# In the second group of quarter tiles, w2 of the second next tile is requested behind a visit at an iteration's fourth hook

## The chip, the cores and the metric

The kernel runs on one core of a Trainium2 chip. Its time is device microseconds (us) of one execution, and the median of several executions is compared. TensorE (PE in the profile, PEld for its weight loads), VectorE (DVE), ScalarE (ACT) and GpSimd (POOL) compute; SyncE (SP) issues nearly all loads, one after the other in the order of the program.

## The reference, cut to what matters

```
x   = retention(q, k, v)                                    # 2 x 768 tokens, 8 heads of 64
h   = relu(x @ w_in);  x = (h * sigmoid(conv3(h))) @ w_out  # 512 -> 1024 -> 512
e   = argmax(x @ w_gate), or the expert of the token before where the local gate is >= 0.5
out = softmax(x @ w_gate)[e] * (relu(x @ w1[e]) @ w2[e])    # 8 experts, 512 -> 1024 -> 512
```

Only the last line, the experts, is touched by the change.

## The kernel before, in words

After retention, the feed-forward layer and the routing, the 1536 tokens lie in HBM (`xs`), and tables tell which token goes to which expert. An expert's tokens are cut into full tiles of 128 rows, and what is left over into quarter tiles of 32 rows. For these inputs that makes 11 full tiles, whose experts are, in the order of the tiles, 0, 5, 0, 4, 1, 4, 1, 3, 1, 3, 1, and 8 quarter tiles in two groups of four. A group is handled as one tile of 128 rows in which each quarter has another expert's weights.

**Full tiles.** `fetch(j, which)` requests an expert's w1 (`which` 0) or w2 (`which` 1) for tile j: four requests of 512 KB by SP into a raw buffer (`r` in the profile). There are four raw buffers, one for each kind and each parity of j, so tile 7 takes those of tile 5. From tile 2 on a request carries a condition: if the tile has the expert of the tile two before it, the weights are there already, and nothing is moved. With the list above that holds for tiles 2, 5, 6, 8, 9 and 10; tile 7 (expert 3, after expert 4) is loaded. A request that moves nothing still stands in SP's queue and keeps its place in the order. `cut(j, which, i)` splits half of a raw buffer into a high and a low part, twice ACT (L738) and twice DVE (L739) on 1024 columns, into the next of four slots (`ws0h`, `ws0l`, `ws1h`, `wc`). TensorE then multiplies three times for each product (L134 to L136): `g1` with w1, `relu` on ACT (L878), `turn_h` transposes (L826) and splits (L830, L831), `g2` with w2, `finish` scales on ACT (L894) and scatters the rows (L895).

**Groups.** `group(g)` is a generator. Its eight weight pieces of 2 MB, four of w1 and four of w2, are requested by `fetch_q` (L729), four requests of 512 KB each, alternately into two buffers (`qc` and `qs1l`). A piece is requested when TensorE has used up the piece two before it, which had the same buffer. The first two pieces of the second group are requested by the first group.

**The order around the change** is written out by hand. In iteration j of `experts` TensorE does `g1` of tile j+1 and `g2` of tile j, each in two halves, and after each half `hook()` counts one more; iteration j has hooks 3+4j to 6+4j. `QT` lists the hooks at which the group at hand is visited, that is, runs on to its next `yield`:

```
QT = [3, 5, 10, 10, 11, 15, 20] + [21, 26, 30, 30, 31, 35, 40]
```

For the second group this means: at hook 26 (iteration 5, the fourth hook) TensorE multiplies with w1 pieces 0 and 1, and pieces 2 and 3 are requested; at hook 30 (iteration 6, the fourth) it multiplies with pieces 2 and 3, and two pieces of w2 are requested; then, still at hook 30, ACT does the group's relu (L930); at hook 31 the group is transposed (L826, L936, L938); at hooks 35 and 40 it is multiplied with w2 (L946).

In iteration j, between `g1` and `g2`, w2 of tile j+2 is requested (`fetch(j + 2, 1)`). Half by half it is cut one iteration later, behind the halves of `g2`: ACT and DVE work on w2 of tile 7 in iteration 6, and `g2` uses it in iteration 7.

SP takes its queue strictly in order. Before a `fetch` it loads the expert and the condition from a table (L696, L712). Each request waits until the buffer is free, and, since eight semaphores take turns, until the request eight places before it has landed. PSUM has four banks `tp`/`y` (`psb`) that take turns as well.

Of the kernel before, what the change touches and what calls it, by code (L numbers as in the profile page):

```python
# [92 lines left out]
def tile_kernel(ctx, tc, cat, cst, qT, kT, kN, vN, w_in, conv_w, w_out, wg, w1, w2, out):  # L93
# [601 lines left out]
    def expert_at(n):  # L695
        return sy.value_load(ei[0:1, 0, n:n + 1], min_val=0, max_val=E - 1)  # L696

    def raw(lane, which):
        if (lane, which) not in RAW:
            RAW[lane, which] = (wx if lane and which else ws).tile([P, 4, 1024], F32, name=f"r{lane}{which}")  # L700
        return RAW[lane, which]

    def fetch(j, which, parts=range(4)):

        src = (w1, w2)[which].rearrange("e p a n -> e p (a n)")
        kw = {}
        if j == 0:
            src = src[0]
        else:
            src = src[bass.ds(expert_at(j), 1)].rearrange("o p n -> (o p) n")  # L710
            if j > 1:
                kw = dict(cond=sy.value_load(ei[0:1, 1, j:j + 1], min_val=0, max_val=1), cond_hint=True)  # L712
        dst = raw(j % 2, which)
        for i in parts:
            sy.dma_start(out=dst[:, i, :], in_=src[:, i * 1024:(i + 1) * 1024], **kw)

    def fetch_q(g, which, i, parts=range(4)):

        if (g, which, i) not in QW:
            tag = QSLOT[nq[0] % 2]  # L720
            nq[0] += 1
            QW[g, which, i] = home(tag).tile([P, 4, 1024], F32, tag=tag, name="q" + tag)
        w = QW[g, which, i]
        src = (w1, w2)[which].rearrange("e p a n -> e p (a n)")
        for u in parts:
            if (g, u) not in QE:
                QE[g, u] = expert_at(NTILE + 4 * g + u)
            one_e = src[bass.ds(QE[g, u], 1)].rearrange("o p n -> (o p) n")
            sy.dma_start(out=w[:, u, :], in_=one_e[:, i * 1024:(i + 1) * 1024])  # L729

    def cut(j, which, i):

        tag = SLOT[ncut[0] % len(SLOT)]
        ncut[0] += 1
        w = home(tag).tile([P, 2, 2, 1024], F32R, tag=tag, name="w" + tag)
        for h in range(2):
            r = RAW[j % 2, which][:, 2 * i + h, :]
            se.activation(out=w[:, 0, h, :], in_=r, func=AF.Copy)  # L738
            ve.tensor_tensor(out=w[:, 1, h, :], in0=r, in1=w[:, 0, h, :].bitcast(F32), op=ALU.subtract)  # L739
        W[j, which, i] = w.rearrange("p s h n -> p s (h n)")  # L740
# [3 lines left out]
    def gather(j, n=NT):  # L744

        X[j] = xg = xpool[0].tile([P, DM], F32, name="xg")
        po.memset(xg, 0.0)
        return po.indirect_dma_start(out=xg, out_offset=None, in_=xs[0:n], in_offset=bass.IndirectOffsetOnAxis(ap=it[:, j:j + 1], axis=0),  # L748
                                     bounds_check=n - 1, oob_is_err=False)
# [86 lines left out]
    def begin_x(j):  # L836

        x, X[j] = X[j], psb.tile([P, 4, P], F32, tag="b", name="tp")
        for k in range(4):
            te.matmul(X[j][:, k, :], x[:, k * P:(k + 1) * P], ident, start=(k == 0), stop=False, skip_group_check=True)  # L840
        late_x(j, 0)
# [6 lines left out]
    def turn_x(j):  # L848

        if j < 2:  # L850
            late_x(j, 1)
        hi, lo = (wk.tile([P, 4, P], F32R, name="x" + n) for n in "hl")
        x = X.pop(j)
        ps = x if j < 2 else turn(x, 0)
        split(ps, hi, lo)
        XT[j] = hi, lo

    def turn_h(j):

        t = [wk.tile([P, 8, P], F32R, name="t" + n) for n in "hl"]  # L860
        hr = HR.pop(j)
        ps = [turn(hr, i) for i in (0, 4)]
        for i in (0, 4):
            split(ps[i // 4], t[0][:, i:i + 4, :], t[1][:, i:i + 4, :])
        return t

    def g1(j, i, h):
        xh, xl = XT[j]
        w = W.pop((j, 0, i))
        for n in range(2):  # L870
            for k in (2 * i, 2 * i + 1):
                o = slice((k % 2) * F + n * 512, (k % 2) * F + (n + 1) * 512)
                mm3(h[n], xh[:, k, :], xl[:, k, :], w[:, 0, o], w[:, 1, o], k == 0, k == 3)

    def relu(j, h):
        HR[j] = hr = wk.tile([P, F], F32, name="hr")
        for n in range(2):
            se.activation(out=hr[:, n * 512:(n + 1) * 512], in_=h[n], func=AF.Relu)  # L878

    def g2(j, i, t, y):  # L880
        hh, hl = t
        w = W.pop((j, 1, i))
        for k in range(4 * i, 4 * i + 4):
            o = slice((k % 4) * DM, (k % 4 + 1) * DM)
            mm3(y, hh[:, k, :], hl[:, k, :], w[:, 0, o], w[:, 1, o], k == 0, k == 7)

    def finish(j, last=False):
        if last:
            yo = wk.tile([P, F], F32, tag="hr", name="yo")[:, 0:DM]
        elif j >= NTILE:  # L890
            yo = wk.tile([P, F], F32, tag="hq", name="yo", bufs=1)[:, 0:DM]
        else:
            yo = wk.tile([P, DM], F32, name="yo", bufs=1)
        se.activation(out=yo, in_=Y.pop(j), func=AF.Copy, scale=pr[:, j:j + 1])  # L894
        po.indirect_dma_start(out=rows_of[j], out_offset=bass.IndirectOffsetOnAxis(ap=it[:, j:j + 1], axis=0),  # L895
                              in_=yo, in_offset=None, bounds_check=NT - 1, oob_is_err=False)

    def tile_g1():
        return [psa.tile([P, 512], F32, tag=f"a{n}", name="g1") for n in range(2)]
# [55 lines left out]
    QT = [3, 5, 10, 10, 11, 15, 20] + [21, 26, 30, 30, 31, 35, 40]  # L955
    groups = []
    hooks = [0]

    def hook():
        hooks[0] += 1  # L960
        while QT and QT[0] <= hooks[0]:
            QT.pop(0)
            while groups and next(groups[0], done) is done:
                groups.pop(0)

    def experts(n):

        fetch_q(0, 0, 1)
        fetch(1, 1)
        for j in range(2):  # L970
            begin_x(j)
        for j in range(2):
            turn_x(j)
        gather(NTILE)
        gather(2)
        groups.extend(group(g, g + 1 < QSTAT) for g in range(QSTAT))
        h = tile_g1()
        for i in range(2):
            g1(0, i, h)
            cut(1, 0, i)  # L980
            if i:
                relu(0, h)
            hook()
        cut(0, 1, 0)
        fetch(2, 0)
        T = {}
        for j in range(n):
            last, ahead = j + 1 == n, j + 2 < n
            behind = j + 3 < n and j > 0 and hooks[0] + 1 in QT
            if j + 3 < n and not behind:  # L990
                fetch(j + 3, 0)
            if j > 0:
                finish(j - 1)
            if j + 3 < n:
                gather(j + 3)
            if j == 2:
                gather(NTILE + 1)
            if j not in T and j > 0:
                T[j] = turn_h(j)
            if not last:  # L1000
                h = tile_g1()
                g1(j + 1, 0, h)
                if j == 0:
                    T[j] = turn_h(j)
                    cut(0, 1, 1)
                if ahead:
                    cut(j + 2, 0, 0)
                hook()
                if behind:
                    fetch(j + 3, 0)  # L1010
                g1(j + 1, 1, h)
                if ahead:
                    cut(j + 2, 0, 1)
                relu(j + 1, h)
                hook()
            if ahead:
                turn_x(j + 2)
                fetch(j + 2, 1)
            Y[j] = y = psb.tile([P, 512], F32, tag="b", name="y")
            for i in range(2):  # L1020
                g2(j, i, T[j], y)
                if not last:
                    cut(j + 1, 1, i)
                    if not ahead and i == 0:
                        T[j + 1] = turn_h(j + 1)
                    hook()
        finish(n - 1, True)
        assert not QT

    def lone(j):  # L1030
# [15 lines left out]
        finish(j)  # L1046

    experts(NSTAT)
    value = lambda n, top: nc.values_load(ei[0:1, 0, n:n + 1], min_val=0, max_val=top)
    with tc.If(value(N_MORE, 1) > 0):  # L1050
# [47 lines left out]
```

## Time and profile before

| | us |
|---|---|
| median of 3 runs | 422.44 (422.02 to 424.92) |
| the profiled execution | 423.74 |
| its span, first to last instruction | 421.9 |
| mean granted clock of TensorE | 0.996 of full speed |

The profiled execution is 1.8 us longer than its span and 1.3 us longer than the median of the runs. In the timeline a row merges instructions of one line that follow each other; `x4` is their number. For SP a row's start is when the first request was issued, which is when its waits were over. Of the weight loads, a request that moves 512 KB is seen with an issue of 0.33 us and more, one whose condition is false with 0.07 to 0.08 us. Since a request waits for the landing of the one eight places before, an issue that had waited marks that landing.

### The profile page before, as it was taken

The numbers are of one execution on the slowest core, as the hardware profiler recorded it, in microseconds if no ns is written. First come the engines' busy times: TensorE is split into PE (matmuls) and PEld (weight loads), VectorE is DVE, ScalarE is ACT, GpSimd is POOL, SyncE is SP. The second block draws the span as 40 slices with busy tenths as digits, with TensorE's granted clock in tenths as the row PEclk, the third lists the DMA queues.
The fourth block names the chain that finished last, engine by engine and source line by source line (L and its number), as shares of the span: only waits on it lengthen the run. The fifth ranks groups of instructions, "written<-read, shape, count | busy, mean of one in ns | idle before, by whom it ended". The sixth has DMA issues, their size and how long they took to land.

```text
span 421.9 us, 7069 instructions
## 1 busy us (share of the span) xinstructions
PE 406.2 (96%) x2412; PEld 329.5 (78%) x2412; DVE 290.3 (69%) x494; ACT 256.1 (61%) x405; POOL 92.7 (22%) x92
## 2 busy tenths in 40 slices
PE   8999999999999999999999999999999998999992
PEld 7898999999987889988778886767667764676671
DVE  3789989798973621678995387968595957285550
ACT  2787778578663333667313487869586846485550
POOL 5356756230100000000004130341131320200110
PEclk9999999999999999999999999999999999999998
DMA  7989871320000101000486999999978969658301
GB/s 238 389 295 405 276 246 54 106 89 6 2 2 0 75 27 50 2 0 2 174 294 198 372 406 331 381 412 401 403 285 302 361 244 402 237 218 299 151 31 42
DMA packets 27322, 86.57 MB, mean 205 GB/s; under 512 B 3598, under 2 KB 4622, under 8 KB 27280
## 3 DMA queue, kind: packets, MB, share of 16 engines
q1 hardware_dynamic: 25200, 79.76, 51.1%
q0 software_dynamic: 2080, 6.29, 4.1%
q8 instruction: 21, 0.34, 0.3%
q14 instruction: 21, 0.17, 0.1%
HBM read 105.18 MB, written 6.55 MB: 265 GB/s over the span
## 4 chain that ended last, share of the span: by engine, by line
PE 38%; issue 34%; POOL 10%; DVE 8%; ACT 4%; DMA 3%; SPq 1%; POOLq 0%
PE x_ps L134 6%; PE x_ps L135 5%; PE x_ps L136 5%; POOL out_dram L895 4%; POOL xg L748 4%; PE h_ps L134 3%; PE y L304 3%; PE h_ps L135 3%; PE s_ps L284 3%; PE h_ps L136 3%; DVE cc L367 3%; DMA xs<-xl 2%; PE y L306 2%; DMA kq<-in_qT_dram 1%; ACT cc L364 1%
## 5 line engine op out<-in xcount | busy, mean ns | idle before, releaser
L134 PE MATMUL h_ps<-xT,wih 128*128 128x384 f32 x128 | 46.1, 360 | 0.1
L895 POOL DMA_INDIRECT out_dram<-yo,it x13 | 16.4, 1262 | 134.8 <-ACT yo L894 134.8
L367 DVE SCALAR_TENSOR_TENSOR cc<-h,cw,cc 128x768 f32<-128x768 f32 x32 | 34.9, 1091 | 15.2 <-ACT cc L364 15.1
L748 POOL DMA_INDIRECT xg<-xs,it x13 | 18.4, 1418 | 121.8 <-DVE ei L683 107.9
L135 PE MATMUL h_ps<-xT,wih 128*128 128x384 f32 x128 | 43.1, 337 | 0.0
L136 PE MATMUL h_ps<-xT,wil 128*128 128x384 f32 x128 | 43.1, 336 | 0.0
L134 PE MATMUL x_ps<-woh,hg 128*128 128x512 f32 x96 | 38.6, 402 | 0.0
L135 PE MATMUL x_ps<-wol,hg 128*128 128x512 f32 x96 | 37.5, 391 | 0.0
L136 PE MATMUL x_ps<-woh,hg 128*128 128x512 f32 x96 | 37.5, 391 | 0.0
L739 DVE TENSOR_TENSOR ws1h<-r,ws1h 128x1024 fp32r<-128x1024 f32 x22 | 26.0, 1222 | 12.8 <-ACT ws1h L738 9.3
L155 POOL TENSOR_TENSOR na<-na,raw 128x512 int32<-128x512 int32 (+1 forms) x17 | 23.0, 1354 | 50.8 <-DVE na L153 25.7
L739 DVE TENSOR_TENSOR wc<-r,wc 128x1024 fp32r<-128x1024 f32 x22 | 26.0, 1221 | 11.7 <-ACT wc L738 11.6
L738 ACT ACTIVATE wc<-r 128x1024 fp32r<-128x1024 f32 x22 | 22.1, 1055 | 14.6 <-PE g L136 14.6
L304 PE MATMUL y<-at,vz 128*128 128x128 f32 x192 | 29.5, 275 | 0.9 <-ACT vz L279 0.9
L284 PE MATMUL s_ps<-qz,kq 128*128 128x256 f32 x96 | 29.0, 385 | 1.0 <-DVE qz L253 1.0
L739 DVE TENSOR_TENSOR ws0h<-r,ws0h 128x1024 fp32r<-128x1024 f32 x22 | 26.0, 1222 | 5.6 <-ACT ws0h L738 5.5
L739 DVE TENSOR_TENSOR ws0l<-r,ws0l 128x1024 fp32r<-128x1024 f32 x22 | 26.0, 1222 | 5.1 <-ACT ws0l L738 5.0
L304 PEld LDWEIGHTS y<-at,vz 128*128 128x128 f32 x192 | 25.9, 192 | 1.5 <-ACT vz L279 1.1
L738 ACT ACTIVATE ws0l<-r 128x1024 fp32r<-128x1024 f32 x22 | 22.1, 1053 | 7.7 <-PE y L136 7.7
L286 DVE TENSOR_TENSOR at<-s_ps,ca 128x256 f32<-128x256 f32 x48 | 20.2, 421 | 8.4 <-PE s_ps L284 7.7
L134 PEld LDWEIGHTS h_ps<-xT,wih 128*128 128x128 f32 x128 | 24.1, 189 | 1.9 <-issue 1.2
L506 ACT ACTIVATE xn<-x_ps 128x512 f32<-128x512 f32 x10 | 6.0, 598 | 32.0 <-PE x_ps L136 13.8
(234 smaller groups left out, 1042.4 us busy)
## 6 DMA issues: line engine op xcount, KB each, us to landing
r<-in_w_dram SPq DMA_DIRECT2D x88, 512.0 KB
qc<-in_w_dram SPq DMA_DIRECT2D x32, 512.0 KB
qs1l<-in_w_dram SPq DMA_DIRECT2D x32, 512.0 KB
raw<-in_w_in_dram SPq DMA_DIRECT2D x8, 512.0 KB
raw<-in_w_out_dram SPq DMA_DIRECT2D x8, 512.0 KB
kq<-in_qT_dram SPq DMA_DIRECT2D x7, 384.0 KB
kq<-in_kT_dram SPq DMA_DIRECT2D x7, 384.0 KB
kv<-in_vN_dram SPq DMA_DIRECT2D x7, 384.0 KB
```

What stands on the lines that cost most here:

```text
L134: te.matmul(ps, lhi, rhi, start=first, stop=False)
L135: te.matmul(ps, lhi, rlo, start=False, stop=False)
L136: te.matmul(ps, llo, rhi, start=False, stop=last)
L155: po.tensor_tensor(out=a, in0=a, in1=lo, op=ALU.add)
L284: te.matmul(ps, self.kq[:, 0, tok], self.qz[:, :, tok], start=True, stop=True)
L286: ve.tensor_tensor(out=self.at[c], in0=ps, in1=self.dm, op=ALU.mult)
L304: te.matmul(y, vz[:, c, j, :], at[:, j, :], start=(j == 0), stop=(c == 0 and j == 1))
L367: ve.scalar_tensor_tensor(out=cc, in0=h[:, i:i + S], scalar=cw[:, m, i:i + 1], in1=cc, op0=ALU.mult, op1=ALU.add)
L738: se.activation(out=w[:, 0, h, :], in_=r, func=AF.Copy)
L739: ve.tensor_tensor(out=w[:, 1, h, :], in0=r, in1=w[:, 0, h, :].bitcast(F32), op=ALU.subtract)
L748: return po.indirect_dma_start(out=xg, out_offset=None, in_=xs[0:n], in_offset=bass.IndirectOffsetOnAxis(ap=it[:, j:j + 1], axis=0), bound ...
L895: po.indirect_dma_start(out=rows_of[j], out_offset=bass.IndirectOffsetOnAxis(ap=it[:, j:j + 1], axis=0), in_=yo, in_offset=None, bounds_ch ...
```

## The change

Where the second group is the one at hand, the next hook is not in `QT` and the one after it is, `fetch(j + 2, 1)` moves from ahead of `g2` to behind the iteration's fourth hook. The condition is true in iterations 5 (hook 26) and 6 (hook 30).

```
             if ahead:
                 turn_x(j + 2)
-                fetch(j + 2, 1)
+                after = len(groups) == 1 and hooks[0] + 1 not in QT and hooks[0] + 2 in QT
+                if not after:
+                    fetch(j + 2, 1)
             Y[j] = y = psb.tile([P, 512], F32, tag="b", name="y")
             for i in range(2):
                 g2(j, i, T[j], y)
                 if not last:
                     cut(j + 1, 1, i)
                     if not ahead and i == 0:
                         T[j + 1] = turn_h(j + 1)
                     hook()
+            if ahead and after:
+                fetch(j + 2, 1)
```

Only SP's queue changes; the other engines' instructions stand as before. In iteration 5 SP has, before the change, w1 of tile 8 (`r00`), w2 of tile 7 (`r11`) and then the second group's third piece of w1 (`qc4`) and the fourth (`qs1l`):

```order
L715 DMA r00_2027<-in_w1_dram 128x1024
L696 TENSOR_LOAD ei_1427
L696 ISA x2
L712 TENSOR_LOAD ei_1427
L712 ISA x2
L715 ISA
L715 DMA r11_2465<-in_w2_dram 128x1024
...
L729 DMA qc4_3689<-in_w1_dram 128x1024
...
L729 DMA qs1l_3702<-in_w1_dram 128x1024
```

And with the change, at the same place:

```order
L715 DMA r00_2027<-in_w1_dram 128x1024
L729 ISA
L729 DMA qc4_3667<-in_w1_dram 128x1024
...
L729 DMA qs1l_3680<-in_w1_dram 128x1024
...
L696 TENSOR_LOAD ei_1427
L696 ISA x2
L712 TENSOR_LOAD ei_1427
L712 ISA x2
L715 ISA
L715 DMA r11_2465<-in_w2_dram 128x1024
```

The eight requests of the group's pieces now stand ahead of the four of tile 7's w2 and of the table loads that belong to them. In iteration 6 SP has, before the change, w1 of tile 9 (`r10`), w2 of tile 8 (`r01`) and the group's first two pieces of w2:

```order
L715 DMA r10_2037<-in_w1_dram 128x1024
...
L715 DMA r01_2032<-in_w2_dram 128x1024
...
L729 DMA qc4_3868<-in_w2_dram 128x1024
...
L729 DMA qs1l_3881<-in_w2_dram 128x1024
```

And with the change:

```order
L715 DMA r10_2037<-in_w1_dram 128x1024
...
L729 DMA qc4_3846<-in_w2_dram 128x1024
...
L729 DMA qs1l_3859<-in_w2_dram 128x1024
...
L715 DMA r01_2032<-in_w2_dram 128x1024
```

Here too the group's eight requests move ahead of four requests; those four move nothing with these inputs.

## Rows read from the trace of the kernel before

**Rows 1.** Page, part 1: busy us, share of the span, instructions of each engine

```profile
PE 406.2 (96%) x2412; PEld 329.5 (78%) x2412; DVE 290.3 (69%) x494; ACT 256.1 (61%) x405; POOL 92.7 (22%) x92
```

**Rows 2.** Waits of TensorE, 240 to 422 us: total us, times, longest

```profile
PE hq_ps L924 <- DMA qs1l<-in_w_dram: 1.2, 2, 1.0
...
PE hq_ps L924 <- DMA qc<-in_w_dram: 0.2, 1, 0.2
```

**Rows 3.** Timeline of TensorE, first group's visit at hook 10: start, us

```profile
273.76 1.92 PE L924 MATMUL hq_ps<-qc,xq 128*32 128x512 f32 x16
...
277.33 1.09 PE L826 MATMUL tp<-cs,hr 128*128 128x128 f32 x8
```

**Rows 4.** Timeline of TensorE, second group's visits at hooks 26, 30 and 31

```profile
337.70 2.80 PE L924 MATMUL hq_ps<-qs1l,xq 128*32 128x512 f32 x16
...
352.84 1.83 PE L924 MATMUL hq_ps<-qc,xq 128*32 128x512 f32 x6
...
358.20 2.15 PE L924 MATMUL hq_ps<-qs1l,xq 128*32 128x512 f32 x4 [0.98 <-DMA qs1l<-in_w_dram]
...
362.38 1.09 PE L826 MATMUL tp<-cs,hr 128*128 128x128 f32 x8
...
366.07 1.03 PE L826 MATMUL tp<-cs,hq 128*128 128x128 f32 x8
366.86 0.48 PE L134 MATMUL g<-wc,xh 128*128 128x512 f32 x1
```

**Rows 5.** Timeline of SP's requests, iterations 4 to 6: start, us to the last issue

```profile
325.93 0.33 SPq L729 DMA_DIRECT2D qs1l<-in_w_dram  x1
...
338.67 0.07 SPq L715 DMA_DIRECT2D r<-in_w_dram  x1
340.35 2.45 SPq L715 DMA_DIRECT2D r<-in_w_dram  x4
343.09 2.44 SPq L729 DMA_DIRECT2D qc<-in_w_dram  x4
345.79 4.29 SPq L729 DMA_DIRECT2D qs1l<-in_w_dram  x4
351.63 9.06 SPq L715 DMA_DIRECT2D r<-in_w_dram  x8
...
354.96 0.07 SPq L715 DMA_DIRECT2D r<-in_w_dram  x1
...
360.62 0.07 SPq L715 DMA_DIRECT2D r<-in_w_dram  x1
360.94 1.93 SPq L729 DMA_DIRECT2D qc<-in_w_dram  x4
```

**Rows 6.** Windows: length, busy us (count) by engine, clock, DMA share, GB/s

```profile
338.00:341.00 3.00, 3.00 (x21) 0.94 (x16) 1.52 (x2) 0.65 (x2) 2.02 (x2) 1.00 0.03 10
341.00:342.00 1.00, 1.00 (x8) 0.92 (x7) 0.24 (x1) 0.87 (x2) 0.79 (x1) 1.00 0.96 258
342.00:358.00 16.00, 14.99 (x68) 9.47 (x67) 11.18 (x11) 9.59 (x12) 0.26 (x1) 1.00 1.01 398
```

**Rows 7.** Timeline of ACT, iterations 6 and 7

```profile
350.38 2.01 ACT L738 ACTIVATE ws0h<-r 128x1024 fp32r<-128x1024 f32 x2
...
352.94 2.00 ACT L738 ACTIVATE ws0l<-r 128x1024 fp32r<-128x1024 f32 x2 [0.55 <-PE y L136]
362.49 1.09 ACT L930 ACTIVATE hq<-hq_ps 128x512 f32<-128x512 f32 x2 [7.54 <-PE hq_ps L924]
363.46 0.69 ACT L894 ACTIVATE yo<-y,pr 128x512 f32<-128x512 f32 x1
364.03 1.10 ACT L830 ACTIVATE th<-tp 128x512 fp32r<-128x512 f32 x2
366.27 2.01 ACT L738 ACTIVATE ws1h<-r 128x1024 fp32r<-128x1024 f32 x2 [1.14 <-PE g L136]
...
373.22 2.01 ACT L738 ACTIVATE ws0h<-r 128x1024 fp32r<-128x1024 f32 x2
```

More of the change, by code (lines that the diff above doesn't have):

```diff
@@ L1017, in experts @@
                 turn_x(j + 2)
-                fetch(j + 2, 1)
+                after = len(groups) == 1 and hooks[0] + 1 not in QT and hooks[0] + 2 in QT
+                if not after:
+                    fetch(j + 2, 1)
             Y[j] = y = psb.tile([P, 512], F32, tag="b", name="y")
@@ L1026, in experts @@
                     hook()
+            if ahead and after:
+                fetch(j + 2, 1)
         finish(n - 1, True)
```

## The prediction

> **What bounds the kernel now.** The page's first part comes first: TensorE is busy for 96% of the span [rows 1]. That bounds the kernel only on the whole, because matmul ends are modelled and a wait inside a row can hide. So I read TensorE's waits in the experts' part next: nearly all of them are for the group's w1 pieces, two for `qs1l` and one for `qc`, but only 1.4 us in total [rows 2]. The timeline tells more. The first group's visit that multiplies with pieces 2 and 3 (hook 10) takes from 273.76 to 277.33 us, 3.57 us until the next transposes [rows 3]. The second group's same visit (hook 30) takes from 352.84 to 362.38, 9.54 us, for the same instructions [rows 4]. So 5.97 us of it are a stall, four times what the wait list shows, and ACT's relu of the group waits 7.54 us for TensorE there [rows 7].
>
> Why the pieces come late is seen in SP's rows [rows 5]. At 338.67 SP issues the last of eight requests that move nothing, which marks the landing of the group's request issued at 325.93. Only then tile 7's four w2 requests go out, from 340.35, then `qc` from 343.09 and `qs1l` from 345.79. From 351.63 to 360.62 the next eight empty requests each mark a landing of `qc` and `qs1l`: seven intervals in 8.99 us, 1.28 us for 512 KB or 408 GB/s. `qc` is complete at 354.96, `qs1l` at 360.62, against a visit that begins at 352.84. The windows show that this is a matter of order and of a late start, not of a train that is too long: from 338 to 341 the DMA engines are 3% busy, from 342 to 358 they are full at 398 GB/s [rows 6]. Tile 7's w2, which goes first, is in no hurry: ACT cuts it from 350.38 to 354.94 [rows 7], and TensorE uses it an iteration later, behind 366.86 [rows 4].
>
> **The change, part by part.**
>
> *The group's eight requests go first.* No table load stands between the last empty request and `qc`, as none does at 360.62, where `qc` follows in 0.32 us, to 360.94 [rows 5]. So `qc` goes out at 338.67 + 0.32 = 338.99, 1.36 us before the train of twelve starts today. `qc` is free by then, and `qs1l` when TensorE is through with it, at 337.70 + 2.80 = 340.50 [rows 4], which is about when its turn comes: four `qc` requests took 1.93 us from 360.94, so 340.92. SP does not stand still there. Today the train's eighth request lands at 354.96, 14.61 us behind the start at 340.35; with the change the eighth is the last of `qs1l`, and lands at 338.99 + 14.61 = 353.60. The visit begins at 352.84, and reaches `qs1l` after half of 3.57 us, at 354.6. Nothing waits, and the visit ends at 352.84 + 3.57 = 356.41: 5.97 us gained so far.
>
> *Tile 7's w2 goes last, and a new wait comes of it.* Its fourth request is the train's twelfth. That one lands at 360.62 today, 20.27 us behind the start, and would land at 338.99 + 20.27 = 359.26. Its table loads cost nothing: they are done while SP waits for landings anyway. But ACT runs in order, and the cut of w2 stands ahead of the group's relu, of `yo` of tile 6 and of the split of tile 7 [rows 7]. Its last instruction starts at about 359.3; the next starts 0.95 us behind (a pair takes 2.01 us, each 1.05), so the relu starts at 360.25. From 362.49 to the end of `yo` at 364.15 pass 1.66 us, so `yo` ends at 361.9. TensorE is at the transposes of the group earlier: from 362.38 to 366.07 it needs 3.69 us, so it gets there at 356.41 + 3.69 = 360.1. The first four transposes need the relu; the last four take the bank that `yo` empties. They end some 0.45 us behind `yo` (half of 366.07 to 366.86, and a semaphore), and the next matmul starts at 362.36 instead of 366.86. So 4.50 us are left of the 5.97; the new wait is 1.5 us.
>
> One thing shifts the train a little. POOL's transfers around 341 to 342 (258 KB in that 1 us [rows 6]) run today before the train is in motion, and would now share with it: 0 to 0.6 us at 398 GB/s. I take 0.1, near the lower end, since most of it passes while the new train, too, has only just begun: 4.4 us.
>
> *Behind it* nothing gives this back. ACT today waits 1.14 us for TensorE before the first cut of iteration 7 [rows 7], and a lag of ACT behind TensorE ends at its next such cut, where it waits for a slot that TensorE frees. The group's first w2 piece, today requested from 360.94 [rows 5], can go once TensorE has used `qc` (354.6) and tile 7's w2 lands, from 355 on, one request a landing; it is sooner than today, as is the visit at hook 35.
>
> *In iteration 6* the four requests of tile 8's w2 that move behind the group move no bytes, but the cut that reads them waits for them all the same: today it starts at 373.22 [rows 7], with the change at about 368.8. They wait in turn for the landings of the group's first w2 piece, issued from 355 to 359.5. At 1.28 us a request behind 359.26 that piece lands by 365, and the four cost nothing. The upper bound is the longest time from issue to landing in these rows, 338.67 - 325.93 = 12.7 us: then it lands at 372, and ACT loses up to 3 us. I take 0.
>
> *The sum*: 5.97 - 1.47 - 0.1 = 4.4 us, so the profiled execution goes from 423.74 to 419.3, and the median from 422.44 to **418.0 us**. That is 1.04%, close to the 1% that I take as what a measurement of this kernel can tell from no change.
>
> The Trainium skill, "DMA: Bandwidth & Descriptors", section "Bandwidth", says that for transfers from HBM to SBUF one core's share of the HBM, about 358 GB/s, binds. By that figure, as an estimate, the twelve requests would take 17.6 us instead of 15.4, w2 would land 2.2 us later and 2.2 us of gain be left. This trace does not agree: 398 GB/s for 16 us, and 408 from landing to landing.
>
> **The rivals.**
>
> 1. *The whole stall is gained.* The new wait vanishes if w2's last request lands by 357.8, so that `yo` ends when TensorE arrives. For: empty time and 1.28 us a request. Against: the same train took 20.27 us, and 18.8 would be needed. 422.44 - 5.97 = 416.5 us. 12%.
> 2. *A longer new wait.* w2's last request waits for the landing of the one eight before, 338.99 + (349.7 - 340.35) = 348.4 by today's train. If it then takes the 12.7 us seen for the request of 325.93, it lands at 361.1, and 2.6 us are left: 419.8; the cases from 1 to 3.7 us belong here. 17%.
> 3. *The wait only changes its place.* The DMA engines are full for the whole train, and whoever is last waits. If w2 lands at about 363.7, the next matmul starts where it starts today: 422.4 us. Against: today the last to land is wanted by TensorE at once, whereas w2 is wanted by ACT, with 4.5 us between. 9%.
> 4. *Slower: ACT's queue blocks the group and tile 7 at once.* Behind the late cut stand the relu, `yo` and the split of tile 7. From a landing of 363.8 on every us of w2 is a us of TensorE. That takes SP held up at `qs1l`: if TensorE's visit at hook 26, which is itself fed by a piece landing at 338.67, ended 7 us later relative to SP, w2 would land at 366 and the median be 424.7. Against: TensorE is through at 340.50. 7%.
>
> That the change doesn't do what it says is excluded by the order: the eight requests stand ahead of the four in both places.
>
> **How the numbers follow.** The forecast, a gain of 3.7 to 5.2 us, has 55%, the rivals 12, 17, 9 and 7%. Its own range is 417.2 to 418.7. Rivals 1 and 2 belong to the range of 8 in 10: from 416.4 to 421.0, the end of a small part of rival 2 left out. A gain of 1% is 4.2 us: of the forecast some 38 of 55 lie above it, since its middle does, and all of rival 1. So faster by over 1% has 50%, within 1% 44% (the rest of the forecast, rivals 2 and 3, and 1 of rival 4), slower 6%.
>
> **What would show it.** In the trace after, SP's `qc` and `qs1l` go out from about 339.0 and tile 7's w2 behind them; the visit that begins at 352.8 lasts some 3.6 us; ACT's cut `ws0h`, `ws0l` of w2 ends at about 360.3 instead of 354.9, and TensorE waits for ACT at the group's transposes for 1 to 2 us. From 367 us on all rows stand 4 to 4.5 us earlier than today. Wrong would be a visit that still waits for `qs1l` (the train starts no sooner), a cut that ends behind 361.5 (w2 lands later), or rows that lose the lead again by hook 35 or 40.

## The result, and the profile after

The median went from 423.6 us (22 runs) to 419.7 us (22 runs), a ratio of 0.9914 with a 95% interval of 0.9892 to 0.9936: a gain of 2.7 to 4.6 us. The profiled execution's span is 416.8 us, against 421.9. Only part of that difference of 5.1 us belongs to the change, as the timeline shows. Of the runs behind this document one, of e3 (422.05 us), was in a slower state and is left out of e3's median below.

TensorE's timeline after, from the second group's visit at hook 30 to the transposes of tile 9's x, which stand behind the second half of `g1`:

```profile
351.89 1.92 PE L924 MATMUL hq_ps<-qc,xq 128*32 128x512 f32 x16
353.63 2.11 PE L924 MATMUL hq_ps<-qs1l,xq 128*32 128x512 f32 x16
355.68 1.09 PE L826 MATMUL tp<-cs,hr 128*128 128x128 f32 x8
...
360.54 0.66 PE L826 MATMUL tp<-cs,hq 128*128 128x128 f32 x4 [1.02 <-ACT hq L930]
361.60 0.66 PE L826 MATMUL tp<-cs,hq 128*128 128x128 f32 x4 [0.41 <-ACT yo L894]
362.01 0.47 PE L134 MATMUL g<-wc,xh 128*128 128x512 f32 x1
...
364.86 0.60 PE L826 MATMUL tp<-cs,xg 128*128 128x128 f32 x4
```

These rows answer to [rows 4]. The visit takes 355.68 - 351.89 = 3.79 us instead of 9.54, near the first group's 3.57 [rows 3]; and where before nothing was waited for ahead of the group's transposes, TensorE now waits for ACT, once for the group's relu and once for `yo`. From the visit's start to the transposes of x pass 12.97 us. Before, that row was

```profile
369.68 0.60 PE L826 MATMUL tp<-cs,xg 128*128 128x128 f32 x4
```

which is 369.68 - 352.84 = 16.84 us behind the visit's start. The place of the change thus gives 3.87 us, about what the median moved. Of the rest of the 5.1 us, 0.95 lie ahead of the visit (it starts at 351.89 instead of 352.84), where the programs are the same or wait for transfers requested earlier, and 0.28 behind 364.86, all of it after TensorE's last matmul.

SP's requests after, answering to [rows 5]; the rows of one request mark landings:

```profile
337.73 0.07 SPq L715 DMA_DIRECT2D r<-in_w_dram  x1
338.05 1.96 SPq L729 DMA_DIRECT2D qc<-in_w_dram  x4
340.26 2.09 SPq L729 DMA_DIRECT2D qs1l<-in_w_dram  x4
344.43 3.48 SPq L715 DMA_DIRECT2D r<-in_w_dram  x4
...
353.92 0.07 SPq L715 DMA_DIRECT2D r<-in_w_dram  x1
...
358.94 0.33 SPq L729 DMA_DIRECT2D qc<-in_w_dram  x1
```

`qc` follows the last empty request in 0.32 us, and tile 7's w2 now goes last. At 353.92 an empty request of tile 9 has waited for the last request of `qs1l`, at 358.94 the group's first w2 piece for the last of tile 7's w2. And ACT, answering to [rows 7]:

```profile
355.19 2.26 ACT L738 ACTIVATE ws0h<-r 128x1024 fp32r<-128x1024 f32 x2 [5.63 <-DMA r<-in_w_dram]
357.75 2.25 ACT L738 ACTIVATE ws0l<-r 128x1024 fp32r<-128x1024 f32 x2 [0.30 <-DMA r<-in_w_dram]
359.90 1.07 ACT L930 ACTIVATE hq<-hq_ps 128x512 f32<-128x512 f32 x2
360.86 0.69 ACT L894 ACTIVATE yo<-y,pr 128x512 f32<-128x512 f32 x1
...
365.06 2.01 ACT L738 ACTIVATE wc<-r 128x1024 fp32r<-128x1024 f32 x2 [0.16 <-PE g L136]
```

The wait has changed its engine: ACT now waits 5.63 us for w2, and the relu, whose input is there from 355.7, stands behind it until 359.90. TensorE is at the group's transposes before that.

### The profile page after: what moved, and what is told of

Same layout as the page of the kernel before. It is cut to its first block, busy times and chain, and to the rows that moved or that the text cites. A ratio compares the mean times of both kernels' runs of the same rounds, so it can differ in the third digit from the quotient of the medians.

```text
span 416.8 us, 7069 instructions
## 1 busy us (share of the span) xinstructions
PE 401.9 (96%) x2412; PEld 329.5 (79%) x2412; DVE 290.1 (70%) x494; ACT 256.3 (61%) x405; POOL 93.2 (22%) x92
## 4 chain that ended last, share of the span: by engine, by line
PE 39%; issue 33%; POOL 10%; DVE 8%; DMA 4%; ACT 3%; SPq 1%; POOLq 0%
PE x_ps L134 6%; PE x_ps L136 5%; PE x_ps L135 5%; POOL xg L748 4%; POOL out_dram L895 4%; PE h_ps L134 3%; PE y L304 3%; PE h_ps L135 3%; PE h_ps L136 3%; PE s_ps L284 3%; DVE cc L367 3%; PE y L306 2%; DMA kv<-in_kN_dram 2%; DMA xs<-xl 1%; ACT cc L364 1%
## 5 line engine op out<-in xcount | busy, mean ns | idle before, releaser
L738 ACT ACTIVATE ws0h<-r 128x1024 fp32r<-128x1024 f32 x22 | 22.2, 1064 | 7.9 <-DMA r<-in_w_dram 5.6
```

## The experiments

The table gives for each kernel the stretch from the start of the visit at hook 30 to the transposes of tile 9's x. It leaves out what differs between two executions ahead of that place. The ratios are to the kernel before, with 95% intervals. They were taken from the runs and not from the medians shown, and differ from the quotients of those medians by up to 0.3%.

| kernel | visit, us | visit to transposes of x, us | median, us | ratio |
|---|---|---|---|---|
| before | 9.54 | 16.84 | 423.6 | 1 |
| the change | 3.79 | 12.97 | 419.7 | 0.9914 (0.9892 to 0.9936) |
| e1, hook 26 alone | 3.57 | 12.63 | 419.69 | 0.9893 (0.9859 to 0.9927) |
| e2, hook 30 alone | 10.08 | 17.39 | 424.31 | 1.0028 (0.9997 to 1.0059) |
| e3, change, visit first | 3.57 | 10.89 | 417.52 | 0.9877 (0.9829 to 0.9925) |
| e5, w2 early | 4.70 | 12.01 | 419.04 | 0.9877 (0.9837 to 0.9917) |
| e6, w2 twice | 3.57 | 20.23 | 426.18 | 1.0057 (1.0019 to 1.0094) |
| e7, before without w2 | 3.57 | 10.88 | 417.54 | 0.9879 (0.9836 to 0.9921) |
| e8, hook 26 alone, visit first | 3.57 | 10.88 | 417.79 | 0.9865 (0.9826 to 0.9903) |

**e1 and e2: which of the two moves does it.** One move each:

```
e1:  after = len(groups) == 1 and hooks[0] + 1 not in QT and hooks[0] + 2 == 26
e2:  after = len(groups) == 1 and hooks[0] + 1 not in QT and hooks[0] + 2 == 30
```

Expected of e1:

> Only the move at hook 26 (tile 7's w2 behind the group's third and fourth piece of w1); at hook 30 the order of before. Theory (the gain comes from the landing of those w1 pieces ahead of the visit at hook 30): as the full change, a ratio to before of about 0.99, the visit at hook 30 in 3.6 to 3.9 us, the transposes of the group 1 to 2 us late behind ACT. Rival (the earlier request of the group's w2 at hook 30 is what counts): no gain, ratio 1.00, or a wait at hook 35.

Expected of e2:

> Only the move at hook 30 (tile 8's empty w2 requests behind the group's first two pieces of w2); at hook 26 the order of before. Theory: ratio 1.00 within 0.4%, the visit at hook 30 takes 9 to 9.6 us as before. Rival (the earlier request of the group's w2 counts): a ratio of 0.99 and a visit at hook 35 or 40 that is shorter than before.

TensorE in e1:

```profile
354.19 1.92 PE L924 MATMUL hq_ps<-qc,xq 128*32 128x512 f32 x16
...
357.76 1.09 PE L826 MATMUL tp<-cs,hr 128*128 128x128 f32 x8
362.50 0.66 PE L826 MATMUL tp<-cs,hq 128*128 128x128 f32 x4 [0.88 <-ACT hq L930]
363.56 0.66 PE L826 MATMUL tp<-cs,hq 128*128 128x128 f32 x4 [0.41 <-ACT yo L894]
366.82 0.60 PE L826 MATMUL tp<-cs,xg 128*128 128x128 f32 x4
```

and in e2:

```profile
352.44 1.89 PE L924 MATMUL hq_ps<-qc,xq 128*32 128x512 f32 x6
...
358.14 1.05 PE L924 MATMUL hq_ps<-qs1l,xq 128*32 128x512 f32 x2 [1.26 <-DMA qs1l<-in_w_dram]
...
362.52 1.09 PE L826 MATMUL tp<-cs,hr 128*128 128x128 f32 x8
...
369.83 0.60 PE L826 MATMUL tp<-cs,xg 128*128 128x128 f32 x4
```

e1 has the whole effect, the short visit and the wait for ACT behind it; e2 keeps the stall and gains nothing. The move at hook 30 is without effect here. The visit of e2 was expected at 9 to 9.6 us and took 10.08: the last of its twelve requests landed 20.8 us behind the first one's issue, against 20.27 before.

**e3 and e8: taking the new wait away.** In iteration 6 the visit and the scaling of tile 6 stand ahead of the second cut; e3 has both moves, e8 that at hook 26 alone. `finish` of tile 6 is then left out where it stood, at the start of iteration 7:

```
-if j > 0:
+if j > 0 and j - 1 in Y:
     finish(j - 1)
 ...
 g2(j, i, T[j], y)
+early = hooks[0] + 1 == 30
+if early:
+    hook()
+    finish(j)
 if not last:
     cut(j + 1, 1, i)
     ...
-    hook()
+    if not early:
+        hook()
```

Expected of e3:

> The full change, and in iteration 6 the visit at hook 30 and the scaling of tile 6 stand ahead of ACT's second cut of tile 7's w2, so that the group's relu and yo no longer wait for that w2. Theory (what is missing of the stall's 5.97 us is the wait for ACT behind the late cut): TensorE's waits of 1.0 and 0.4 us before the group's transposes are gone, and the kernel is 1.2 to 1.5 us faster than the full change. Rival (the wait moves on: the cut then ends later and the second half of g2 of tile 7 waits for it): the same time as the full change within 0.3 us.

Expected of e8:

> The move at hook 26 alone, and the visit at hook 30 and the scaling of tile 6 ahead of ACT's second cut of tile 7's w2. Theory: no wait of TensorE for w1 pieces or for ACT, 10.9 us from the visit's start to the next transposes of x, ratio 0.986 to 0.988, 1 to 1.5 us better than the change. Rival (the move at hook 30 has a part in it): slower than with both moves, a wait at hook 35.

ACT and TensorE in e3:

```profile
356.13 1.07 ACT L930 ACTIVATE hq<-hq_ps 128x512 f32<-128x512 f32 x2
357.08 0.69 ACT L894 ACTIVATE yo<-y,pr 128x512 f32<-128x512 f32 x1
357.65 2.01 ACT L738 ACTIVATE ws0l<-r 128x1024 fp32r<-128x1024 f32 x2
```

```profile
351.18 1.92 PE L924 MATMUL hq_ps<-qc,xq 128*32 128x512 f32 x16
...
354.75 1.09 PE L826 MATMUL tp<-cs,hr 128*128 128x128 f32 x8
358.46 1.03 PE L826 MATMUL tp<-cs,hq 128*128 128x128 f32 x8
362.07 0.60 PE L826 MATMUL tp<-cs,xg 128*128 128x128 f32 x4
```

and in e8:

```profile
352.83 1.92 PE L924 MATMUL hq_ps<-qc,xq 128*32 128x512 f32 x16
...
363.71 0.64 PE L826 MATMUL tp<-cs,xg 128*128 128x128 f32 x4
```

The waits are gone, the cut of w2 ends at 359.66 in e3, and TensorE waits for nothing later on its account: 2.08 us less than with the change in this stretch, 10.89 against 12.97, in e8 10.88. Expected of e3 were 1.2 to 1.5 us, the two waits alone; the visit, 0.22 us shorter, and the transposes, which run as one group again, 0.3 us shorter, come on top. Against before that is 16.84 - 10.89 = 5.95 us, all of the stall of 5.97. Both kernels beat the change in their medians, by 2.2 and 1.9 us, although the kernel before was 0.3 us slower beside them (423.9 us). They did not run beside the change; e1, which has its waits and did run beside e3, has 419.69 us. The intervals overlap in both comparisons, so the timing alone does not settle it; the stretch does.

**e7: without tile 7's w2.** The order of before, and

```
-fetch(j + 2, 1)
+if j != 5:
+    fetch(j + 2, 1)
```

Expected:

> The kernel before, without the four requests of tile 7's w2; tile 7 uses what its buffer holds (expert 4's w2), so 2 MB and their place in SP's queue are left out. Theory (these four requests ahead of the group's pieces are the whole cause of the stall, and behind them, of the change's new wait): the visit at hook 30 in 3.6 to 3.9 us, no wait for ACT at the transposes, from the visit's start to the next transposes of x some 10.9 us (16.84 before, 12.97 with the change), ratio to before about 0.986. Rival (SP's empty requests hold up the pieces as well): a stall of 1 us or more is left.

```profile
350.12 1.92 PE L924 MATMUL hq_ps<-qc,xq 128*32 128x512 f32 x16
...
353.69 1.09 PE L826 MATMUL tp<-cs,hr 128*128 128x128 f32 x8
...
361.00 0.60 PE L826 MATMUL tp<-cs,xg 128*128 128x128 f32 x4
```

Without these four requests there is no stall and no wait for ACT, and the stretch is that of e3 and e8 to 0.01 us. So there is no stall without the four requests ahead of the group's pieces; the eight empty requests, which still stand there, cost nothing by themselves. That the four go out only behind the empty ones has its part in the stall all the same, as e5 shows.

**e5: w2 early instead of late.** The order of before, but at the start of iteration 5

```
+if j == 5:
+    fetch(j + 2, 1)      # tile 7's w2, before: behind g1 of iteration 5
+    fetch(j + 1, 1)      # empty, before: iteration 4
```

and the empty `fetch(8, 0)` behind hook 26. Expected:

> The order of before with one other edit: at the start of iteration 5 tile 7's w2 is requested first, ahead of the empty requests of tiles 6 (w2) and 8 (w1), of which the latter go behind the group's pieces at hook 26. Nothing is late then for ACT, and the DMA engines have no empty stretch from 338 to 341 us. Theory (the stall is one of order and of a late start of the train, not of its length): the visit at hook 30 takes under 4.5 us, no wait of TensorE for ACT at the transposes, 5 to 6 us faster than before, that is about 1 us faster than the change. Rival (the DMA engines are full and whoever is last is waited for): the visit at hook 30 still waits for qs1l for 2 us or more, and the gain is 3 us or less.

```profile
327.71 3.85 SPq L715 DMA_DIRECT2D r<-in_w_dram  x4
...
340.44 4.01 SPq L729 DMA_DIRECT2D qc<-in_w_dram  x4
344.71 2.09 SPq L729 DMA_DIRECT2D qs1l<-in_w_dram  x4
```

```profile
353.40 1.92 PE L924 MATMUL hq_ps<-qc,xq 128*32 128x512 f32 x16
355.14 3.03 PE L924 MATMUL hq_ps<-qs1l,xq 128*32 128x512 f32 x16
358.10 1.09 PE L826 MATMUL tp<-cs,hr 128*128 128x128 f32 x8
...
365.41 0.60 PE L826 MATMUL tp<-cs,xg 128*128 128x128 f32 x4
```

```profile
348.78 2.01 ACT L738 ACTIVATE ws1h<-r 128x1024 fp32r<-128x1024 f32 x2 [6.02 <-DMA r<-in_w_dram]
```

The w2 requests go out at 327.71, while the empty ones would hold SP up, and use the time in which the DMA engines stood empty: from 338 to 340 us they move 412 GB/s, where before they were 3% busy from 338 to 341. TensorE's wait for ACT is gone, but `qc` can only go as w2 lands, a request a landing, and the second half of the visit waits 1.1 us for `qs1l` (3.03 us instead of 1.90). The visit was expected under 4.5 us and took 4.70. So the order still counts for 1.1 us, even with the early start, against what I expected. Of the stall of 5.97 us 4.83 are gone from the stretch. The edit has a price of its own on ACT: tile 8's w1, whose empty requests now stand behind the group's, is cut only after a wait of 6.02 us, which ACT has made up by the group's relu.

**e6: w2 twice.** The change, with tile 7's w2 requested twice, the second time behind the landing of the first:

```
 if ahead and after:
-    fetch(j + 2, 1)
+    for _ in range(2 if j == 5 else 1):
+        fetch(j + 2, 1)
```

Expected:

> The full change, with tile 7's w2 requested twice at hook 26: each second request of the same 512 KB waits for the landing of the first, so the weights that ACT's cut waits for land some 3 to 4 us later. Theory (ACT's late cut stands ahead of the group's relu and of yo, and TensorE waits for both): the visit at hook 30 still takes 3.6 to 3.9 us, TensorE's wait for ACT at the group's transposes grows from 1.4 us to about 5, and every us of w2 is a us of the kernel, so that the gain is gone: ratio to before 0.998 to 1.003. Rival (ACT and DVE have slack there, w2 is wanted only an iteration later): ratio as the full change, 0.990.

```profile
352.67 1.92 PE L924 MATMUL hq_ps<-qc,xq 128*32 128x512 f32 x16
...
356.24 1.09 PE L826 MATMUL tp<-cs,hr 128*128 128x128 f32 x8
366.29 2.18 PE L826 MATMUL tp<-cs,hq 128*128 128x128 f32 x8 [6.19 <-ACT hq L930]
372.90 0.60 PE L826 MATMUL tp<-cs,xg 128*128 128x128 f32 x4
```

The visit is as short as ever, TensorE's wait for ACT grows to 6.2 us, and the kernel is slower than before: more than expected, which was a wait of about 5 us and a ratio of 0.998 to 1.003. ACT's relu starts 12.99 us behind the visit's start (365.66 - 352.67) instead of 8.01: 5.0 us later. The stretch is 7.3 us longer. TensorE reaches the end of its wait 5.0 us later too; the other 2.3 us lie behind it, where the granted clock was at half, as is told at the end. This is the prediction's fourth rival, made on purpose.

## Why the prediction was right

**The mechanism held step by step.** The stall was four times what the wait list showed, and all but 0.2 us of it goes: 9.54 to 3.79 us with the change, 3.57 in e1. `qc` went out 0.32 us behind the last empty request, as taken. The new wait came where it was put, at the group's transposes, in two parts, behind the relu and behind `yo`. ACT caught up in iteration 7, at the second cut instead of the first, where it waits 0.16 us for TensorE; the lead of 4.82 us that TensorE has at the transposes of x (369.68 - 364.86) is still there at its last matmul; and iteration 6's move was worth nothing (e2). e7 shows that there is no stall without the four requests, e3 and e8 that the missing part is the wait for ACT, e6 that every later us of w2 is paid.

**One size was off, the landing of w2,** so that 3.9 us came instead of 4.4. "*Tile 7's w2 goes last*" put the train's twelfth landing 20.27 us behind its start, from one train of one execution. The change's train took 358.94 - 338.05 = 20.89 us, 0.62 more. What hangs on it came as the prediction has it: the matmul behind the group's transposes starts 362.01 - 351.89 = 10.12 us behind the visit's start, where 362.36 - 352.84 = 9.52 were taken. Before, it started 366.86 - 352.84 = 14.02 us behind it. So 3.90 us are gained there instead of 4.50, and the new wait, by the prediction's measure, is 2.07 us instead of 1.47. The waits listed for ACT are 1.43 us of it; the others are 0.22 us in the visit, 0.3 us for transposes that no longer run as one group, and 0.1 us that no wait shows.

The eighth landing was late as well, 353.92 - 338.05 = 15.87 us behind the start instead of 14.61, so that the visit waited 0.2 us for `qs1l` after all. The prediction had named such a wait as a sign of being wrong, for a train that starts no sooner; here the train started as taken and was slower. The wait cost nothing more, since ACT was later still: in e1 the visit waits for nothing, and from the start of ACT's relu to the transposes of x pass 366.82 - 361.87 = 4.95 us, with the change 364.86 - 359.90 = 4.96.

In e1, e3 and e8 the twelfth landed 20.7, 20.4 and 20.7 us behind the start, and in e2, with the order of before, 20.8. The term's spread over these six trains is thus some 0.6 us, and the one train that the prediction used was the shortest. The term for POOL's transfers, 0.1 of a possible 0.6 us, had a reason that failed, that most of them pass while the new train has only just begun. Before, POOL's queue moved 0.26 of 0.52 MB from 340 to 342, ahead of the train's bytes; with the change all 0.52 MB move from 343 to 348, in a train in full motion. The 0.26 MB more are 0.6 us at 408 GB/s, as much as w2 was late. But in e2, where POOL's first half goes ahead as before, the twelfth landed no earlier, so how much of the delay is POOL's stays open.

**The time itself** was put at 418.0 us, and at 417.2 to 418.7 for the forecast alone; it came out at 419.7, inside the range of 8 in 10 (416.4 to 421.0). Of the 1.7 us 1.2 are the kernel before, whose median was 422.44 us in three runs and 423.6 in 22. The gain lies inside the forecast's 3.7 to 5.2 us, near its lower end. It is 0.86%, with an interval of 0.64 to 1.08%: on the side of 1% to which the prediction gave the smaller chance, 44% against 50%, and the interval reaches over 1%.

**The clearest rival** was the whole stall gained. It did not come, because w2's last request landed 20.89 us behind the train's start, where 18.8 would have been needed, and ACT's order let nothing pass; e3 shows that it takes only another order on ACT. Rival 3, a wait that only changes its place, is true to a third: 2.1 of the 5.95 us. The sentence against it, that w2 is wanted by ACT with time between, holds for w2 itself but not for what stands behind its cut.

The Trainium skill's page "TensorE: Matmul & The Clock Gate" says, in its section "Part 1: The HAM clock gate", that an idle engine falls to half its clock. In the change's trace it does not come to that: the waits are 1.0 and 0.4 us, and the granted clock stays at 1.00 from 350 to 370 us. e6's trace agrees with the page, with a clock of 0.50 behind a wait of 6.2 us.

## What to carry to other kernels

A load that goes out early because it can, ahead of one that is wanted sooner, can make the second late by its own length, as tile 7's four requests did here. Order requests by when they are wanted, and count what an in-order engine has queued behind the consumer of the one that is put last: here that cost a third of the stall's 6 us, and taking the group's relu and `yo` ahead of the waiting cut gave it back. The wait list showed 1.4 us of a stall of 5.97; comparing the same step in two places of the timeline showed all of it.

## What the runs showed of the hardware

In these runs one wait of about 6 us cost more than the same time in pieces. In the kernel before, the stall of 5.97 us came with matmuls in between, as each request landed, and the granted clock stayed at 1.00. The windows of before give length, busy us (count) of PE, PEld, DVE, ACT, POOL, then clock, DMA share and GB/s:

```profile
356.00:360.00 4.00, 2.96 (x8) 0.41 (x6) 0.39 (x1) 0.00 (x0) 0.00 (x0) 1.00 0.63 249
360.00:364.00 4.00, 3.80 (x22) 1.88 (x22) 0.00 (x0) 1.51 (x3) 0.00 (x0) 1.00 0.46 130
```

In e6 TensorE stood still for 6.2 us on end, and its windows are:

```profile
360.00:366.00 6.00, 0.10 (x1) 0.00 (x0) 3.78 (x4) 4.47 (x5) 0.00 (x0) 0.67 0.91 311
366.00:368.00 2.00, 1.71 (x7) 1.36 (x8) 1.19 (x2) 2.00 (x5) 0.42 (x1) 0.50 1.02 385
...
370.00:372.00 2.00, 2.00 (x6) 1.61 (x5) 2.00 (x3) 0.66 (x2) 1.41 (x1) 0.50 0.97 338
372.00:374.00 2.00, 2.00 (x11) 1.62 (x11) 0.22 (x1) 0.90 (x1) 0.00 (x0) 0.93 1.03 418
```

The clock is at its lower level, 1.2 of 2.4 GHz, from within the wait until about 372. From the group's transposes to those of x pass 372.90 - 366.29 = 6.61 us instead of 3.61: 3.0 us on top of the wait. With the change, whose waits are 1.0 and 0.4 us, the same two places are 4.32 us apart, at a clock of 1.00, so e6 is 2.3 us behind the change there.
